# A decode block's weights loaded with two and nine rows per partition, and features taken two apart

## The chip, the cores and the metric

The kernel runs on one core of a Trainium2 chip. The metric is device time in microseconds for one execution: the median of several runs. Times inside a run are microseconds from the start of the profiled span.

## The reference

Four sequences (B = 4) decode one token each. D = 576 features, 32 query heads and 16 key/value heads of 128, of the caches only the last 4096 positions, F = 4608 hidden units. In short:

```python
xn = layernorm(x)
q  = xn @ wq                              # [4, 576] x [576, 4096]
p  = softmax(q . k_cache[last 4096] * 128**-0.5)
o  = p @ v_cache[last 4096]
h  = x + o @ wo                           # [4, 4096] x [4096, 576]
hn = layernorm(h)
g, u = hn @ W_gate, hn @ W_up             # [4, 576] x [576, 4608]
out  = h + (relu(g) * u) @ W_down         # [4, 4608] x [4608, 576]
```

All inputs and the output are bf16. Nearly all the bytes are K and V: 64 pairs of a sequence and a key/value head, 2 MB for two of them.

## The kernel before

Every engine has its program written out by hand (`prog_sync`, `prog_pool`, `prog_act`, `prog_dve`, `prog_pe`). `Sched` turns names of steps into semaphore waits; the order of an engine is the order of its program.

**Transfers.** `transfers` is one list that SP issues in order: wq, then K and V of the 32 "duos" (two heads of one sequence, 2 MB each, K five ahead of V), then wo in 4 pieces, gate and up in alternation, W_down in 9 pieces. All land in one large SBUF tile, `pool`. `add` finds whose place a transfer takes, and SP waits for the last reader of that place before it issues. W_down waits for the step ATTN, the end of the wo matmuls.

**Start.** x is normalised, transposed on TensorE in 5 chunks of features (4 of 128 and one of 64), and multiplied by wq: chunk c of features stands against rows 128c to 128c+127 of wq, which lie one to a partition. The last 64 rows lie as halves on 128 partitions (`xn4`, `hn4` hold the input for them).

**Attention.** For each duo VectorE transposes K (`tr`), TensorE makes scores (`qk`) and, later, P times V (`pv`); four duos form a batch with one softmax.

**End.** The wo matmuls (L578) give h transposed, feature chunk n on partitions, 4 columns for the sequences. After the second norm, gate and up: for each feature chunk c and each of 36 groups of 128 hidden units, one matmul loads a 128x128 block of weights from `pool` as the stationary operand and streams hnT's 4 columns (L595). Which 128 hidden units form group f is told by `cols` (L586): units stand JJ = 3 apart, so that a partition of W_down's tile holds JJ rows that follow one another in memory. Chunk 4 has 18 matmuls for each of gate and up, on halves.

Then h is added to the output in PSUM by multiplying R_sb (h transposed) with an fp32 identity (L610), in pieces along the feature chunks and the two halves of the output (288 columns each, one PSUM bank each). Last come 72 matmuls with W_down as moving operand, 288 columns each (L618), whose pieces are listed in `WD` (L235):

```python
wd_sb = pool[:, 0:FC * D].rearrange("p (g x) -> p g x", g=NG)
WD = [(0, GD * JJ), (GD * JJ, 2 * GD * JJ)] + [(g * JJ, (g + 1) * JJ) for g in range(2 * GD, NG - 1)] + [(FC - JJ, FC - 1), (FC - 1, FC)]
```

that is columns 0-8, 9-17, then 18-20 and so on by threes to 32, then 33-34 and 35. Every matmul and weight load is recorded under L482, the helper `mm`.

Of the kernel before, what the change touches and what calls it, by code (L numbers as in the profile page):

```python
# [12 lines left out]
B = 4  # L13
D = 576
# [6 lines left out]
F = 4608  # L21
FC = F // 128
# [8 lines left out]
DUO = 2 * WIN * DH // 128  # L31
NKS = 4
NVS = 4
ROW = 4608
GU0 = 24064
# [1 line left out]
NKT = 3  # L37
VLEAD = 5
PVLAG = 5
JJ = 3  # L40
GD = 3
BIG = 1.5e38
NG = FC // JJ
HALF = F // 2
HD = D // 2
# [57 lines left out]
def bass_sequential_preLN__sliding_block_cached__glu_gated_reglu__decode_kernel(  # L103
# [12 lines left out]
    with ExitStack() as es:  # L116
        cnt = [0]

        def sb(name, shape, dt):
            return es.enter_context(nc.sbuf_tensor(name, shape, dt))  # L120
# [3 lines left out]
        ident_b = sb("ident_b", [128, 128], BF16)  # L124
        ident_f = sb("ident_f", [128, 128], FP32)
# [13 lines left out]
        oX = sb("oX", [128, 4, H // 4, B], BF16)  # L139
# [22 lines left out]
        R_sb = sb("R_sb", [128, 2, DC, B], FP32)  # L162
# [9 lines left out]
        pb = [sc[:, i * 512:(i + 1) * 512] for i in range(4)]  # L172
        pb += [es.enter_context(nc.psum_tensor(f"pb{i}", [128, 512], FP32))[:, :] for i in range(4, 8)]
        PVB, OB, QB, QR, TPB = 4, 6, 6, 3, 7
        OSB, WOB, STB, GUB, DNB = 0, 1, 2, 7, 4
        tpv = pb[TPB].bitcast(BF16)
# [6 lines left out]
        at = {}  # L183

        def add(name, key, off, n, consumer, make):

            free = []
            for u in list(users):
                if u[0] < off + n and off < u[1]:
                    if u[2] not in free:  # L190
                        free.append(u[2])
                    if off <= u[0] and u[1] <= off + n:
                        users.remove(u)
            users.append((off, off + n, consumer))
            at[name] = off
            transfers.append((name, key, free, lambda e: make(e, pool[:, off:off + n])))
# [13 lines left out]
                lambda e, o: e.dma_start(out=o, in_=duo(A_v_cache, d)))  # L210

        HQ = H * DH
        for c in range(4):
            add(("wq", c), f"wq{c}", NKS * DUO + c * HQ, HQ, "QMM", lambda e, o, c=c: e.dma_start(out=o, in_=A_wq[c * 128:(c + 1) * 128, :]))
        add(("wq", 4), "wq4", NKS * DUO + 4 * HQ, HQ // 2, "QMM",
            lambda e, o: e.dma_start(out=o, in_=A_wq[512:576, :].rearrange("r (u n) -> (r u) n", u=2)))
        for m in range(NDUO + VLEAD):
# [4 lines left out]
        for g in range(NWO):  # L222
            add(("wo", g), f"wo{g}", g * ROW, ROW, "ATTN",
                lambda e, o, g=g: e.dma_start(out=o.rearrange("p (q x) -> p q x", q=2),
                                              in_=A_wo[g * 1024:(g + 1) * 1024, :].rearrange("(q p e) n -> p q (e n)", q=2, e=4)))
        for c in range(4):
            for k, (kind, W) in enumerate((("wg", B_W_gate), ("wu", B_W_up))):
                add((kind, c), f"{kind}{c}", GU0 + (2 * c + k) * ROW, F, None,
                    lambda e, o, c=c, W=W: e.dma_start(out=o, in_=W[c * 128:(c + 1) * 128, :]))
        for u, (kind, W) in enumerate((("wg", B_W_gate), ("wu", B_W_up))):  # L230
            add((kind, 4), f"{kind}4", GU0 + 8 * ROW + u * HALF, HALF, None,
                lambda e, o, W=W: e.dma_start(out=o, in_=W[512:576, :].rearrange("r (u n) -> (r u) n", u=2)))

        wd_sb = pool[:, 0:FC * D].rearrange("p (g x) -> p g x", g=NG)
        WD = [(0, GD * JJ), (GD * JJ, 2 * GD * JJ)] + [(g * JJ, (g + 1) * JJ) for g in range(2 * GD, NG - 1)] + [(FC - JJ, FC - 1), (FC - 1, FC)]  # L235
        for k, (f0, f1) in enumerate(WD):
            g0, j0 = divmod(f0, JJ)
            g1, nj = (f1 // JJ, JJ) if f1 - f0 >= JJ else (g0 + 1, f1 - f0)
            transfers.append((("wd", k), f"wd{k}", ["ATTN"],
                              lambda e, g0=g0, g1=g1, j0=j0, nj=nj: e.dma_start(  # L240
                                  out=wd_sb[:, g0:g1, j0 * D:(j0 + nj) * D],
                                  in_=B_W_down[g0 * 128 * JJ:g1 * 128 * JJ, :].rearrange("(g p j) n -> p g (j n)", p=128, j=JJ)[:, :, j0 * D:(j0 + nj) * D])))

        def land(name):
            return ("L",) + (name if isinstance(name, tuple) else (name,))
# [232 lines left out]
        def prog_pe(S):  # L478
            t = "tensor"

            def mm(o, l, r, start, stop, deps=(), name=None, skip=False):
                S.op(t, lambda e: e.matmul(o, lhsT=l, rhs=r, start=start, stop=stop, skip_group_check=skip),  # L482
                     deps=deps, name=name, signal=name is not None)

            for k, (src, base) in enumerate(((xn_bf, 0), (x_bf, 32))):
                for c in range(DC):
                    w = 128 if c < 4 else 64
                    last = k == 1 and c == DC - 1
                    S.op(t, lambda e, c=c, w=w, src=src, base=base: e.transpose(  # L489
                        out=tpv[0:w, base + c * 4:base + (c + 1) * 4], in_=src[0:B, c * 128:c * 128 + w], identity=ident_b[0:B, 0:B]),  # L490
                        deps=["A_XN", "IDB", land("x")] if k == 0 and c == 0 else [], name="TP1" if last else None, signal=last)
            mm(pb[STB][:, 0:B], dup[:, :], x4[:, :], True, True, deps=["D_XNT", "DUP"], name="XDUP")
            first = True
            for c in range(4):
                s = at[("wq", c)]
                for h in range(H):
                    mm(pb[QB][:, h * B:(h + 1) * B], pool[:, s + h * DH:s + (h + 1) * DH], xnT[:, c, :], first, False,
                       deps=[land(("wq", c))] + (["D_XNT"] if first else []) if h == 0 else [], skip=True)
                    first = False
            s = at[("wq", 4)]  # L500
            for h in range(H // 2):
                o = pb[QB][:, 0:H * B].rearrange("p (u x) -> p u x", u=2)[:, :, h * B:(h + 1) * B]
                mm(o, pool[:, s + h * DH:s + (h + 1) * DH], xn4[:, :, :], False, h == H // 2 - 1,
                   deps=[land(("wq", 4)), "XN41"] if h == 0 else [],
                   name="QMM" if h == H // 2 - 1 else None, skip=True)
            for ce in range(4):
                mm(pb[QR][:, ce * 128:(ce + 1) * 128], sel[:, ce, :, :].rearrange("p g k -> p (g k)"), qT_sb[:, :], True, True,
                   deps=["D_QT", "SEL3"] if ce == 0 else [], name="QREP" if ce == 3 else None)
# [55 lines left out]
            for e_ in range(4):  # L564
                for h4 in range(4):
                    mm(pb[OSB][32 * h4:32 * h4 + 32, e_ * 32:(e_ + 1) * 32], ident_b[:, e_:128:4],
                       oT_all[:, :, :].rearrange("p (q h) b -> p h q b", h=4)[:, h4, :, :], True, True,
                       deps=[("NORM", b) for b in range(B)] if e_ == 0 and h4 == 0 else [],
                       name="OSEL" if e_ == 3 and h4 == 3 else None)
            for g in range(NWO):  # L570
                wv = pool[:, at[("wo", g)]:at[("wo", g)] + ROW].rearrange("p (q e n) -> p q e n", q=2, e=4)
                deps = [land(("wo", g))] + (["D_OX"] if g == 0 else [])
                for n in range(DC):
                    w = 128 if n < 4 else 64
                    for q in range(2):
                        for e_ in range(4):
                            last = g == NWO - 1 and n == DC - 1 and q == 1 and e_ == 3
                            mm(pb[WOB][0:w, n * B:(n + 1) * B], wv[:, q, e_, n * 128:n * 128 + w], oX[:, e_, 2 * g + q, :],  # L578
                               g == 0 and n == 0 and q == 0 and e_ == 0, last, deps=deps, name="ATTN" if last else None, skip=True)
                            deps = []  # L580
            mm(pb[STB][:, 128:168], ones_f[:, :], R_sb[:, :, :, :], True, True, deps=["D_R"], name="STAT")
            mm(pb[STB][:, 256:256 + B], dup[:, :], hnT[0:64, 4, :], True, True, deps=["N2"], name="HDUP")
            first = True
            gub = pb[GUB][:, 0:2 * FC * B].rearrange("p (u x) -> p u x", u=2)

            def cols(ap, fc):  # L586
                g, j = divmod(fc, JJ)
                x0 = g * 128 * JJ + j
                return ap[:, x0:x0 + 127 * JJ + 1:JJ]

            for c in range(4):
                for u, kind in ((0, "wg"), (1, "wu")):
                    s = at[(kind, c)]
                    for f in range(FC):
                        mm(gub[:, u, f * B:(f + 1) * B], cols(pool[:, s:s + F], f), hnT[:, c, :], first, False,  # L595
                           deps=[land((kind, c))] + (["N2"] if first else []) if f == 0 else [], skip=True)
                        first = False
            for u, kind in ((0, "wg"), (1, "wu")):
                o = gub[:, u, :].rearrange("p (v x) -> p v x", v=2)
                for f in range(FC // 2):  # L600
                    last = u == 1 and f == FC // 2 - 1
                    mm(o[:, :, f * B:(f + 1) * B], cols(pool[:, at[(kind, 4)]:at[(kind, 4)] + HALF], f), hn4[:, :, :], False, last,
                       deps=[land((kind, 4)), "HN41"] if f == 0 else [], name=("GU", 4) if last else None, skip=True)
            first = True
            for u in range(2):
                for c in range(DC):
                    lo, hi = max(c * 128, u * HD), min(c * 128 + 128, D, (u + 1) * HD)
                    if lo < hi:
                        w = 128 if c < 4 else 64
                        mm(pb[DNB + u][0:B, lo - u * HD:hi - u * HD], R_sb[0:w, 0, c, :], ident_f[0:w, lo - c * 128:hi - c * 128],  # L610
                           c * 128 <= u * HD, False, deps=["D_R", "IDF"] if u == 0 and c == 0 else [], skip=True)
            for k, (f0, f1) in enumerate(WD):
                deps = [land(("wd", k))] + (["D_HHT"] if k == 0 else [])
                for f in range(f0, f1):
                    g, j = divmod(f, JJ)
                    for u in range(2):
                        last = f == FC - 1
                        mm(pb[DNB + u][0:B, 0:HD], hhT[:, f, :], wd_sb[:, g, j * D + u * HD:j * D + (u + 1) * HD], False, last,  # L618
                           deps=deps, name=f"DOWN{u}" if last else None, skip=True)
                        deps = []  # L620
# [37 lines left out]
```

## Time and profile before

| | |
|---|---|
| median of 3 runs | 384.58 us (384.58 to 385.41) |
| profiled execution | 385.3 us, its span 383.5 us |
| busy share of the span | PE 75%, weight loads 34%, DVE 52%, ACT 13%, POOL 2% |
| DMA | 159.59 MB on SP's queue, 98.6% of 16 engines' span |
| mean rate over the span | 416 GB/s read from HBM |
| granted TensorE clock, mean | 0.907 |

The shares of busy time are averages over four stages (start, attention, wo, gate/up/down). In the first three the transfers run without a break. "PEld" are weight loads, which overlap matmuls; the mean durations of matmuls in a row hold their pipeline, so the pace of a row is read from its length and its count.

### The profile page before, as it was taken

To read this page: it belongs to the slowest core of one execution; us is meant where nothing else is said; L and a number is where in the kernel's file an instruction comes from. 1 tells how busy PE (TensorE), PEld (TensorE's weight loads), DVE (VectorE), ACT (ScalarE), POOL (GpSimd) and SP (SyncE) were. 2 spreads that over 40 slices of the span, in tenths; PEclk is the share of its full clock that TensorE was granted. 3 is DMA by queue.
4 is the path that set the end of the run, shared out by engine and by line. 5 is a ranking of instruction groups with operands and counts; after the bars stand their busy time and mean duration, and the time that the engine had idled before them with its cause. 6 is when DMAs were issued, how large, how long until landed. Compare 5 with 4: busy or idle time off the path is not lost.

```text
span 383.5 us, 4157 instructions
## 1 busy us (share of the span) xinstructions
PE 288.7 (75%) x1827; PEld 130.2 (34%) x1842; DVE 198.8 (52%) x181; ACT 51.5 (13%) x125; POOL 7.9 (2%) x20
## 2 busy tenths in 40 slices
PE   0059649976996699679958994899499788874387
PEld 0053213322432243224322431343134233374355
DVE  0259789269437854774486558645855450011000
ACT  4021040021102110311030004100400021100000
POOL 4000000000000000000000000000000000000000
PEclk9999958998999899989998999899989998955559
DMA  7999999999999999999999999999999999999994
GB/s 316 426 424 426 431 424 432 426 424 431 426 424 434 424 427 431 426 427 431 426 427 434 424 424 434 427 424 432 427 424 434 426 423 434 403 417 424 414 415 172
DMA packets 14306, 159.86 MB, mean 417 GB/s; under 512 B 1480, under 2 KB 1616, under 8 KB 4560
## 3 DMA queue, kind: packets, MB, share of 16 engines
q1 hardware_dynamic: 14280, 159.59, 98.6%
q8 instruction: 14, 0.23, 0.2%
q10 hardware_dynamic: 8, 0.00, 0.0%
q14 instruction: 4, 0.03, 0.0%
HBM read 159.58 MB, written 0.00 MB: 416 GB/s over the span
## 4 chain that ended last, share of the span: by engine, by line
PE 41%; DMA 23%; issue 15%; DVE 14%; ACT 5%; POOL 1%; SPq 0%; POOLq 0%
PE sc L482 23%; PE pb L482 18%; DMA pool<-in_A_k_cache_dram 9%; DMA pool<-in_B_W_down_dram 7%; DMA pool<-in_A_wo_dram 7%; ACT P L323 4%; DVE kT L394 4%; DVE probT L413 4%; DVE rmx L397 4%; POOL bcm L274 1%; DVE bias L409 0%; DVE rowsum L418 0%; DVE t L405 0%; DVE pmax L400 0%; DVE bmin L407 0%
## 5 line engine op out<-in xcount | busy, mean ns | idle before, releaser
L394 DVE STREAM_TRANSPOSE kT<-pool 128x2048 f32<-128x2048 f32 x64 | 144.5, 2291 | 54.6 <-DMA pool<-in_A_k_cache_dram 49.4
L482 PE MATMUL sc<-kT,qz 128*128 128x512 bf16 x497 | 131.9, 418 | 51.2 <-DVE kT L394 47.6
L482 PE MATMUL pb<-pool,prob 128*16 128x512 bf16 x512 | 116.4, 386 | 0.8 <-DMA pool<-in_A_v_cache_dram 0.8
L482 PEld LDWEIGHTS sc<-kT,qz 128*128 128x128 bf16 x512 | 49.0, 102 | 130.9 <-DVE kT L394 57.0
L482 PEld LDWEIGHTS pb<-pool,prob 128*16 128x16 bf16 x512 | 43.5, 91 | 71.0 <-issue 15.3
L323 ACT ACTIVATE P<-sc,bias 128x512 f32<-128x512 f32 x32 | 22.2, 714 | 176.5 <-DVE bias L409 176.5
L397 DVE TENSOR_REDUCE rmx<-sc 128x2 f32<-128x2048 f32 x8 | 18.3, 2292 | 34.0 <-PE sc L482 34.0
L413 DVE STREAM_TRANSPOSE probT<-P 128x2048 f32<-128x2048 f32 x8 | 18.5, 2311 | 7.8 <-ACT P L323 7.8
L482 PE MATMUL pb<-hnT,pool 128*128 128x4 bf16 x288 | 8.8, 167 | 9.8 <-DMA pool<-in_B_W_up_dram 5.0
L489 PE MATMUL pb<-ident_b,xn_bf 4*128 4x4 bf16 (+1 forms) x5 | 0.4, 175 | 20.3 <-ACT xn_bf L287 20.3
L308 ACT COPY cp<-pb 128x512 f32<-128x512 f32 x8 | 4.7, 584 | 67.5 <-PE pb L482 67.5
L482 PEld LDWEIGHTS pb<-hnT,pool 128*128 128x128 bf16 x288 | 8.2, 104 | 10.3 <-DMA pool<-in_B_W_up_dram 5.2
L422 DVE RECIPROCAL rs_sb<-pb 128x32 f32<-128x32 f32 x4 | 1.4, 338 | 19.8 <-PE pb L482 19.8
L482 PE MATMUL pb<-selT,cp 128*128 128x16 f32 x64 | 7.9, 255 | 4.3 <-ACT cp L308 4.3
L473 DVE TENSOR_TENSOR hhT<-pb,gate_sb 128x144 bf16<-128x144 f32 x1 | 0.3, 308 | 20.9 <-ACT gate_sb L339 20.9
L330 ACT CAST prob<-probT 128x1024 bf16<-128x1024 f32 x8 | 8.4, 1044 | 19.0 <-DVE rs L416 19.0
L482 PE MATMUL pb<-pool,hhT 128*4 128x288 bf16 x72 | 10.5, 315 | 0.4 <-DMA pool<-in_B_W_down_dram 0.4
L482 PEld LDWEIGHTS pb<-selT,cp 128*128 128x128 f32 x64 | 8.2, 191 | 6.3 <-ACT cp L308 5.3
L274 POOL PARTITION_ALL_REDUCE bcm<-pmax x8 | 3.1, 386 | 290.6 <-DVE pmax L400 290.6
L301 ACT COPY qz<-qrep 32x64 bf16<-32x64 bf16 x32 | 7.8, 245 | 7.3 <-DVE qrep L431 7.0
L482 PEld LDWEIGHTS pb<-pool,hhT 128*4 128x4 bf16 x72 | 6.6, 93 | 4.3 <-DMA pool<-in_B_W_down_dram 0.7
L489 PEld LDWEIGHTS pb<-ident_b,xn_bf 4*128 4x128 bf16 (+1 forms) x5 | 0.3, 108 | 20.3 <-ACT xn_bf L287 20.3
(94 smaller groups left out, 71.5 us busy)
## 6 DMA issues: line engine op xcount, KB each, us to landing
pool<-in_A_k_cache_dram SPq DMA_DIRECT2D x32, 2048.0 KB, 28.1
pool<-in_A_v_cache_dram SPq DMA_DIRECT2D x32, 2048.0 KB, 26.1
pool<-in_A_wo_dram SPq DMA_DIRECT2D x4, 1152.0 KB, 21.7
pool<-in_B_W_gate_dram SPq DMA_DIRECT2D x4, 1152.0 KB, 25.7
pool<-in_B_W_up_dram SPq DMA_DIRECT2D x4, 1152.0 KB, 24.5
pool<-in_A_wq_dram SPq DMA_DIRECT2D x4, 1024.0 KB, 7.9
pool<-in_B_W_down_dram SPq DMA_DIRECT2D x2, 1296.0 KB, 27.2
pool<-in_B_W_down_dram SPq DMA_DIRECT2D x5, 432.0 KB, 14.5
```

The lines of the kernel that those rows point to most:

```text
L274: S.op(g, lambda e, n=n: e.partition_all_reduce(bcm[:, n % 2, :], pmax[:, n % 2, :], 128, bass_isa.ReduceOp.max), deps=deps, name=("PAR", n))
L301: S.op(a, lambda e, src=src, dst=dst: e.copy(out=dst, in_=src), deps=deps, name=("QZ", n) if g == 3 else None, signal=g == 3)
L308: S.op(a, lambda e: e.copy(out=cp[:, n % 2, :], in_=pb[PVB + n % 2]), deps=deps, name=("CP", n))
L323: S.op(a, lambda e, n=n, th=th, u=u: e.activation(out=P[:, th * 1024 + u:(th + 1) * 1024:2], in_=sc[:, th * 1024 + u:(th + 1) * 1024:2], f ...
L330: S.op(a, lambda e, n=n: e.copy(out=prob[:, n % 2, :, :, :], in_=probT[:, :, 0:NHB].rearrange("p t (r x) -> p r t x", x=4)), deps=deps, na ...
L394: S.op(v, lambda e: e.transpose(out=dst, in_=src), deps=deps, name=("TR", i))
L397: S.op(v, lambda e: e.tensor_reduce(out=rmx[:, n % 2, :], in_=sc[:, :].rearrange("p (x u) -> p u x", u=2), axis=AX.X, op=ALU.max), deps=[( ...
L413: S.op(v, lambda e: e.transpose(out=probT[:, :, :].rearrange("p t j -> p (t j)"), in_=P[:, :]), deps=[("EXP", n, 1)] + ([("CMP", n - 1)] i ...
L422: S.op(v, lambda e: e.reciprocal(out=rs_sb[:, b, :], in_=pb[OB][:, 64 + b * H:64 + (b + 1) * H]), deps=[("SUM", b)], name=("RS", b))
L473: S.op(v, lambda e: e.tensor_tensor(out=hhT[:, :, :], in0=pb[GUB][:, FC * B:2 * FC * B].rearrange("p (f b) -> p f b", b=B), in1=gate_sb[:, ...
L482: S.op(t, lambda e: e.matmul(o, lhsT=l, rhs=r, start=start, stop=stop, skip_group_check=skip), deps=deps, name=name, signal=name is not None)
L489: S.op(t, lambda e, c=c, w=w, src=src, base=base: e.transpose(out=tpv[0:w, base + c * 4:base + (c + 1) * 4], in_=src[0:B, c * 128:c * 128 ...
```

## The change

wq, gate and up are loaded in pairs of chunks: a transfer takes 256 rows, two neighbouring rows on each partition (wq 16384 bytes a partition, gate and up 18432). The feature chunks follow: chunk c of the first four holds features two apart (`feat`), in the transposes of x, in the columns of wo and in the residual matmuls, which write every second column of the output. W_down's tile has JJ = 9 rows a partition instead of 3, so `cols` takes hidden units nine apart, and its pieces are 0-8, 9-17, 18-26, 27-29, 30-32, 33-34, 35. The order of the matmuls is as before, gate and up of chunk c after one another, but both chunks of a pair wait for one landing. The number of matmuls is the same but for the residual, which has seven instead of six.

```diff
-JJ = 3
-GD = 3
+JJ = 9
...
-        for c in range(4):
-            add(("wq", c), f"wq{c}", NKS * DUO + c * HQ, HQ, "QMM", lambda e, o, c=c: e.dma_start(out=o, in_=A_wq[c * 128:(c + 1) * 128, :]))
+        for c in range(2):
+            add(("wq", c), f"wq{c}", NKS * DUO + 2 * c * HQ, 2 * HQ, "QMM",
+                lambda e, o, c=c: e.dma_start(out=o, in_=A_wq[c * 256:(c + 1) * 256, :].rearrange("(p u) n -> p (u n)", u=2)))
...
-        for c in range(4):
+        for c in range(2):
             for k, (kind, W) in enumerate((("wg", B_W_gate), ("wu", B_W_up))):
-                add((kind, c), f"{kind}{c}", GU0 + (2 * c + k) * ROW, F, None,
-                    lambda e, o, c=c, W=W: e.dma_start(out=o, in_=W[c * 128:(c + 1) * 128, :]))
+                add((kind, c), f"{kind}{c}", GU0 + (4 * c + 2 * k) * ROW, 2 * F, None,
+                    lambda e, o, c=c, W=W: e.dma_start(out=o, in_=W[c * 256:(c + 1) * 256, :].rearrange("(p u) n -> p (u n)", u=2)))
...
-        WD = [(0, GD * JJ), (GD * JJ, 2 * GD * JJ)] + [(g * JJ, (g + 1) * JJ) for g in range(2 * GD, NG - 1)] + [(FC - JJ, FC - 1), (FC - 1, FC)]
+        WD = [(0, 9), (9, 18), (18, 27), (27, 30), (30, 33), (33, 35), (35, 36)]
...
+        def feat(c):
+            return slice(c // 2 * 256 + c % 2, c // 2 * 256 + c % 2 + 255, 2) if c < 4 else slice(512, D)
...
-                        out=tpv[0:w, base + c * 4:base + (c + 1) * 4], in_=src[0:B, c * 128:c * 128 + w], identity=ident_b[0:B, 0:B]),
+                        out=tpv[0:w, base + c * 4:base + (c + 1) * 4], in_=src[0:B, feat(c)], identity=ident_b[0:B, 0:B]),
...
-                s = at[("wq", c)]
+                s = at[("wq", c // 2)] + (c % 2) * HQ
...
-                            mm(pb[WOB][0:w, n * B:(n + 1) * B], wv[:, q, e_, n * 128:n * 128 + w], oX[:, e_, 2 * g + q, :],
+                            mm(pb[WOB][0:w, n * B:(n + 1) * B], wv[:, q, e_, feat(n)], oX[:, e_, 2 * g + q, :],
...
-                    s = at[(kind, c)]
+                    s = at[(kind, c // 2)] + (c % 2) * F
                     for f in range(FC):
                         mm(gub[:, u, f * B:(f + 1) * B], cols(pool[:, s:s + F], f), hnT[:, c, :], first, False,
-                           deps=[land((kind, c))] + (["N2"] if first else []) if f == 0 else [], skip=True)
+                           deps=[land((kind, c // 2))] + (["N2"] if first else []) if f == 0 else [], skip=True)
...
-                    lo, hi = max(c * 128, u * HD), min(c * 128 + 128, D, (u + 1) * HD)
-                    if lo < hi:
-                        w = 128 if c < 4 else 64
-                        mm(pb[DNB + u][0:B, lo - u * HD:hi - u * HD], R_sb[0:w, 0, c, :], ident_f[0:w, lo - c * 128:hi - c * 128],
-                           c * 128 <= u * HD, False, deps=["D_R", "IDF"] if u == 0 and c == 0 else [], skip=True)
+                    w = 128 if c < 4 else 64
+                    ds = range(D)[feat(c)]
+                    mine = [p for p in range(w) if u * HD <= ds[p] < (u + 1) * HD]
+                    if mine:
+                        p0, p1 = mine[0], mine[-1] + 1
+                        step = ds.step
+                        o0 = ds[p0] - u * HD
+                        mm(pb[DNB + u][0:B, o0:o0 + step * (p1 - p0 - 1) + 1:step], R_sb[0:w, 0, c, :], ident_f[0:w, p0:p1],
+                           first, False, deps=["D_R", "IDF"] if u == 0 and c == 0 else [], skip=True)
+                        first = False
```

More of the change, by code (lines that the diff above doesn't have):

```diff
@@ L494, in prog_pe @@
             for c in range(4):
-                s = at[("wq", c)]
+                s = at[("wq", c // 2)] + (c % 2) * HQ
                 for h in range(H):
                     mm(pb[QB][:, h * B:(h + 1) * B], pool[:, s + h * DH:s + (h + 1) * DH], xnT[:, c, :], first, False,
-                       deps=[land(("wq", c))] + (["D_XNT"] if first else []) if h == 0 else [], skip=True)
+                       deps=[land(("wq", c // 2))] + (["D_XNT"] if first else []) if h == 0 else [], skip=True)
                     first = False
@@ L603, in prog_pe @@
                        deps=[land((kind, 4)), "HN41"] if f == 0 else [], name=("GU", 4) if last else None, skip=True)
-            first = True
             for u in range(2):
+                first = True
                 for c in range(DC):
-                    lo, hi = max(c * 128, u * HD), min(c * 128 + 128, D, (u + 1) * HD)
-                    if lo < hi:
-                        w = 128 if c < 4 else 64
-                        mm(pb[DNB + u][0:B, lo - u * HD:hi - u * HD], R_sb[0:w, 0, c, :], ident_f[0:w, lo - c * 128:hi - c * 128],
-                           c * 128 <= u * HD, False, deps=["D_R", "IDF"] if u == 0 and c == 0 else [], skip=True)
+                    w = 128 if c < 4 else 64
[8 more added lines that the diff above has]
+                        first = False
             for k, (f0, f1) in enumerate(WD):
```

## The prediction

> **What bounds the kernel now.** I read the page's DMA rows first, then the end of the chain of waits, then the timeline and the windows of the last 20 us. Lines of the page:
>
> ```profile
> PEclk9999958998999899989998999899989998955559
> DMA  7999999999999999999999999999999999999994
> ...
> q1 hardware_dynamic: 14280, 159.59, 98.6%
> ```
>
> The DMA engines are full from the first microseconds to slice 39, so up to the last 20 us the time is bytes over rate. Engines that wait in the attention stage wait for that stream. What follows the stream is seen in the chain of waits (start, length, what):
>
> ```profile
> 343.77 26.88 DMA pool<-in_B_W_down_dram
> 370.64 0.04 issue
> 370.69 10.55 PE pb L482 x72
> 381.24 0.02 issue
> 381.26 0.45 DVE out_sb L475
> ```
>
> The 72 matmuls of W_down start when its first piece lands (370.64) and then run 10.55 us without a wait on any later piece. The timeline shows what PE does just before (start, length, engine, operation; the last bracket is the idle time and what ended it):
>
> ```profile
> 364.66 1.04 PEld L482 LDWEIGHTS pb<-hnT,pool 128*128 128x128 bf16 x36 [1.75 <-DMA pool<-in_B_W_up_dram]
> ...
> 366.10 0.56 PEld L482 LDWEIGHTS pb<-hn,pool 128*128 128x128 bf16 x18 [0.40 <-DMA pool<-in_B_W_gate_dram]
> ...
> 367.52 0.56 PEld L482 LDWEIGHTS pb<-hn,pool 128*128 128x128 bf16 x18 [0.86 <-DMA pool<-in_B_W_up_dram]
> ...
> 368.10 2.17 PE L482 MATMUL pb<-ident_f,R_sb 128*4 128x128 f32 x12
> ```
>
> Gate and up finish 0.6 us after their last landing, the residual matmuls end at 370.27, and only 0.4 us of PE time is left before the first W_down piece. So PE's slack against the stream in this stage is 0.4 us, and behind it PE is the bound. Windows of the same stretch (window, us, PE, PEld, DVE, ACT, POOL, granted clock, DMA share, GB/s):
>
> ```profile
> 200.00:300.00 100.00, 83.81 (x362) 34.09 (x368) 60.04 (x44) 12.32 (x30) 0.77 (x2) 0.95 1.01 428
> 346.00:366.00 20.00, 8.92 (x289) 8.33 (x289) 1.05 (x6) 0.20 (x1) 0.00 (x0) 0.50 1.01 419
> 368.00:376.00 8.00, 7.58 (x50) 4.36 (x48) 0.31 (x1) 0.29 (x1) 0.00 (x0) 0.63 1.03 414
> ...
> 373.00:374.00 1.00, 1.00 (x7) 0.56 (x5) 0.00 (x0) 0.00 (x0) 0.00 (x0) 0.55 1.01 397
> 374.00:375.00 1.00, 1.00 (x10) 0.70 (x9) 0.00 (x0) 0.00 (x0) 0.00 (x0) 1.00 1.02 414
> ...
> 378.00:380.00 2.00, 2.00 (x19) 1.40 (x17) 0.00 (x0) 0.00 (x0) 0.00 (x0) 1.00 0.29 111
> ```
>
> The clock is 0.50 from 337 to 373.9 and 1.00 after it. With c for a W_down matmul at full clock, 3.21/(2c) + 7.34/c = 72 gives c = 0.124 us, and 0.248 at half clock. Its changes in this trace (59.9, 94.0, 373.9) lie 10 and 82 steps of 3.413 us apart, so the next moment at which it could rise is 377.3.
>
> The profiled execution took 385.3 us, 1.8 more than its span; the median is 384.58, 0.7 less. Sums are made against the profiled one, and the difference is carried over to the median.
>
> **Longer rows, so fewer and larger packets.** K and V rows (16 KB) run at 428 GB/s, gate and up (9216 B) at 419, W_down (mostly 3456 B) at 414, wq (8 KB, 6 to 14 us) at 414 in mean. At 428, wq (4.19 MB) saves 0.3 us, the paired gate and up rows (9.44 MB) 0.4 to 0.5, and the 27 of 36 W_down columns that come in nines (3.98 MB) 0.3. The last large up transfer then lands 0.7 us earlier and the middle of W_down 1.0 earlier. Bounds: nothing (longer rows bring none of it) to 1.5 us (wq at 391 in its worst window). I take 0.7 and 1.0.
>
> **Landing granularity.** The wq pairs cost nothing: in the timeline q's matmuls start at 21.43, behind the normalised x (a ScalarE step that ends at 20.20), and all of wq has landed by 15.5. For the first gate and up pair SP now waits for the PV matmuls of duo 28, whose release let the first up transfer go at 327.8; the wo transfer ahead lands at 342.2, so the stream has some 10 us of cover; without it the gap would be idle stream, one for one. Each gate and up pair is needed only when the whole pair is there. The last up pair lands where up 3 lands now, 364.62, less 0.7: 363.9. Behind that landing stand up 2, gate 3, up 3 (36 loads each) and the halves of chunk 4 (18 each), 144 loads instead of 72 with gaps between them. At today's pace, (1.04 - 0.104)/35 = 26.7 ns a load, they take 3.85 us.
>
> **Reading weights 18 bytes apart.** `cols` takes every ninth element instead of every third. q's loads are contiguous and pace at (3.49 - 0.104)/127 = 26.7 ns; gate's, 6 bytes apart, at 26.7 too. No row has 18 bytes. The other end is a load of as many columns without that speed: eight fp32 loads of 128x128 in 0.97 us (mean 191 ns), (0.97 - 0.19)/7 = 111 ns. The ends are 26.7 and 111. I take their middle in ratio, 54 ns. The 6-byte row is nearer, but a step of three times that width can only add, and a loader that delivers 128 columns in 26.7 ns (4.8 a nanosecond, where the fp32 row has 1.2) has most to lose from scattered reads. The 144 loads on the path then take 7.7 us.
>
> [...]
>
> **Features with a stride of two.** The ten transposes of x and wo's 160 loads read 4 bytes apart, between the two steps that show 26.7: nothing, and wo's last 40 matmuls stand behind a landing at 342.16. The residual matmuls become seven instead of six over the same 576 columns and write PSUM 8 bytes apart; today 2.17 us. VectorE's maximum reads PSUM 8 bytes apart, 2048 elements in 2292 ns, as long as its 2048-element transpose from SBUF (2291), so I take 2.2; the other end is a doubling, 4.4. [...]
>
> **W_down in nines.** Columns 18 to 26 come as one piece, which lands where piece 24 to 27 lands now. Between the first piece (370.64) and the last (380.1, its issue at 367.9 plus 12.2 to land) bytes scale to 377.0 for it, less 1.0 gives 376.0. From there 36 matmuls at 0.124 need until 380.4. That is a floor, not the bound, in what follows.
>
> **The sum.** Up pair landed 363.9, plus 7.7 of loads, 0.1 of the last matmul, 2.2 of residual: W_down starts at 373.9 (its data is there). The clock can rise at 377.3: 13.7 matmuls until then, 58.3 at 0.124 after it, end 384.5 against 381.24. That is +3.3 us: 388.6 for the profiled execution, 387.9 for the median.
>
> **Rivals.** (1) *Wide steps cost nothing* (not slower). Loads stay at 26.7 ns: W_down starts at 363.9 + 3.85 + 2.3 = 370.05; with the clock up at 373.9, 15.5 matmuls at half and 56.5 at full clock end at 380.9, that is -0.3: 384.3. For it speaks that contiguous and 6 bytes pace alike; against it, that nothing reaches 18. It decides the sign below about 35 ns a load. (2) *The slow end*, 111 ns: 16.0 us of loads, W_down from 382.2, 10.5 us of it, +11.5: 396.1. For it speaks only that no row excludes it. (3) *The residual's scattered writes double it*, loads at 26.7: start 372.25, end 382.0 or 383.7 by which of the two moments raises the clock: 385.4 to 387.1. (4) *The stream decides*: wide steps are free and the clock is up before W_down starts, as may be so in the median runs, which lie 0.7 below the profiled one. Then the floor counts: 380.4, or less with 1.5 us saved, -0.8 to -1.3: 383.3 to 383.8. (5) *Packets do not grow*: the largest row of before is 16 KB, and rows of 18432 bytes may be cut; that takes 0.4 us from the gain and is inside the other cases.
>
> **How the numbers follow.** A measurement here can tell about 0.3%, 1.15 us, from no change. Forecast (loads of 40 to 75 ns): 0.50, its own range 385.3 to 391.2 (40 ns: start 372.0, end 381.9; 75 ns: start 377.0, clock up at 380.7, end 387.8). Rival 1: 0.32, mostly within 0.3%. Rival 2: 0.09. Rival 3: 0.03. Rival 4: 0.06, the one that is faster. Slower 0.62, same 0.32, faster 0.06. The range reaches from rival 1's value with some of rival 4 down to 384.0, up to 390.7; outside are rival 2, part of rival 4 and the top of the forecast's range.
>
> **What would show it.** In the timeline of after, the LDWEIGHTS group before the residual matmuls: right if its loads stand about 54 ns apart and W_down's chain piece starts near 374 behind PE, not behind a landing. Wrong if a group of 36 still takes 1.04 us. The residual group tells of rival 3 (2.2 or 4.4 us), the window at 346 to 366 of the rates (428 or 419), the chain's last wait of rival 4 (a W_down landing).

## The result, and the profile after

The changed kernel takes 389.29 us (median of 5, 388.63 to 389.70), the kernel before 384.58 (5 runs, 384.55 to 385.41): ratio 1.011, interval 1.0096 to 1.0123. That is 4.7 us slower. The profiled execution took 389.7 us, with a span of 387.9.

The page's lines of after:

```profile
PEclk9999958985998899989998999899999987955559
DMA  8999999999999999999999999999999999999980
q1 hardware_dynamic: 12616, 159.59, 97.2%
```

The bytes are the same in fewer packets (12616 for 14280, 1664 fewer). By the transfers' shapes 1536 rows fewer are read: 256 of wq, 512 of gate and up, 768 of W_down. Had the rows of 18432 bytes come in two packets each, it would be 1024. (The other 128 are packets under 512 bytes, 1480 before and 1352 after.) The DMA engines are now idle in the last slice, while TensorE works on. The end of the chain of waits (start, length, what):

```profile
333.97 29.99 DMA pool<-in_B_W_up_dram
363.97 0.05 issue
364.01 21.62 PE pb L486 x230
385.63 0.02 issue
385.65 0.44 DVE out_sb L479
```

Where the chain came to its last landing at 370.64, with W_down, it now comes there at 363.97, with the last up pair, and TensorE runs from there to the end without a wait: 21.62 us. The timeline shows what it does:

```profile
364.01 6.56 PEld L486 LDWEIGHTS pb<-hnT,pool 128*128 128x128 bf16 x108 [2.44 <-DMA pool<-in_B_W_up_dram]
...
370.47 2.26 PEld L486 LDWEIGHTS pb<-hn,pool 128*128 128x128 bf16 x36
...
372.74 2.17 PE L486 MATMUL pb<-ident_f,R_sb 128*4 128x128 f32 x14
...
374.84 10.77 PE L486 MATMUL pb<-pool,hhT 128*4 128x288 bf16 x72
```

A load takes (6.56 - 0.16)/107 = 60 ns, where it took 26.7. The 144 loads behind the last up landing last from 364.01 to 372.7, the residual is as long as before (2.17 us), and W_down starts at 374.84 instead of 370.69. The windows:

```profile
6.00:14.00 8.00, 0.00 (x0) 0.00 (x0) 0.00 (x0) 0.00 (x0) 0.00 (x0) 1.00 1.01 427
346.00:366.00 20.00, 13.29 (x214) 13.05 (x215) 0.90 (x6) 0.00 (x0) 0.00 (x0) 0.50 1.00 423
378.00:379.00 1.00, 1.00 (x8) 0.59 (x7) 0.00 (x0) 0.00 (x0) 0.00 (x0) 0.73 0.29 107
```

In these profiles wq runs at 427 GB/s (414 before), gate and up at 423 (419), and the last up transfer lands 0.65 us earlier. The rates do not show that longer rows are faster. In the same windows of the other runs below, wq has 420 and 433 where its rows are as before and 423 to 434 where they are paired, and gate and up have 417 to 420 against 416 to 421. The six runs below that also pair gate and up land the last pair between 363.95 and 364.72, where before has 364.62: between 0.67 us earlier and 0.10 later. The clock rises to full within 378 to 379.

### The profile page after: what moved, and what is told of

Same layout as the page of the kernel before. It is cut to its first block, busy times and chain, and to the rows that moved or that the text cites. A ratio compares the mean times of both kernels' runs of the same rounds, so it can differ in the third digit from the quotient of the medians.

```text
span 387.9 us, 4169 instructions
## 1 busy us (share of the span) xinstructions
PE 307.0 (79%) x1844; PEld 142.3 (37%) x1844; DVE 199.1 (51%) x181; ACT 51.6 (13%) x125; POOL 7.9 (2%) x20
## 2 busy tenths in 40 slices
DMA packets 12642, 159.86 MB, mean 412 GB/s; under 512 B 1352, under 2 KB 1488, under 8 KB 3280
## 3 DMA queue, kind: packets, MB, share of 16 engines
q1 hardware_dynamic: 12616, 159.59, 97.2%
## 4 chain that ended last, share of the span: by engine, by line
PE 53%; DVE 17%; issue 15%; DMA 8%; ACT 6%; POOL 1%; POOLq 0%
PE pb L486 28%; PE sc L486 24%; DMA pool<-in_B_W_up_dram 8%; DVE kT L398 6%; ACT P L327 5%; DVE probT L417 4%; DVE rmx L401 4%; POOL bcm L278 1%; DVE bias L413 0%; DVE rowsum L422 0%; DVE t L409 0%; DVE pmax L404 0%; DVE bmin L411 0%; ACT prob L334 0%; ACT qz L305 0%
## 5 line engine op out<-in xcount | busy, mean ns | idle before, releaser
L486 PE MATMUL sc<-kT,qz 128*128 128x512 bf16 x512 | 138.6, 426 | 44.7 <-DVE kT L398 42.9
L486 PE MATMUL pb<-pool,prob 128*16 128x512 bf16 x512 | 117.8, 390 | 0.0
L486 PEld LDWEIGHTS sc<-kT,qz 128*128 128x128 bf16 x512 | 49.6, 103 | 129.6 <-DVE kT L398 53.3
L486 PEld LDWEIGHTS pb<-pool,prob 128*16 128x16 bf16 x512 | 43.9, 91 | 71.7 <-issue 18.1
L486 PE MATMUL pb<-hnT,pool 128*128 128x4 bf16 x288 | 17.8, 199 | 6.0 <-DMA pool<-in_B_W_up_dram 5.5
L486 PEld LDWEIGHTS pb<-hnT,pool 128*128 128x128 bf16 x288 | 17.5, 159 | 6.2 <-DMA pool<-in_B_W_up_dram 5.7
L486 PE MATMUL pb<-selT,cp 128*128 128x16 f32 x64 | 8.7, 269 | 4.3 <-ACT cp L312 4.3
L486 PEld LDWEIGHTS pb<-selT,cp 128*128 128x128 f32 x64 | 9.0, 208 | 6.3 <-ACT cp L312 5.3
L486 PE MATMUL pb<-pool,hhT 128*4 128x288 bf16 x72 | 10.8, 319 | 0.0
L486 PEld LDWEIGHTS pb<-pool,hhT 128*4 128x4 bf16 x72 | 6.7, 94 | 4.0 <-issue 0.2
```

## The experiments

The ratios are to the kernel before in runs on the same chip.

**1. Hidden units three apart, pairs kept** (`e1_step3`).

```diff
-JJ = 9
+JJ = 3
+GD = 3
...
-        WD = [(0, 9), (9, 18), (18, 27), (27, 30), (30, 33), (33, 35), (35, 36)]
+        WD = [(0, GD * JJ), (GD * JJ, 2 * GD * JJ)] + [(g * JJ, (g + 1) * JJ) for g in range(2 * GD, NG - 1)] + [(FC - JJ, FC - 1), (FC - 1, FC)]
```

> The changed kernel with hidden units three apart again (JJ = 3, W_down's pieces as before); the pairs of wq, gate and up and the features two apart stay. Theory (a weight load with columns 18 bytes apart costs 60 ns instead of 26.7, and 144 of them stand behind the last up pair): groups of 36 loads take 1.04 us again, W_down's matmuls start near 370.1 instead of 374.84, and the time is 384.2 us (383.6 to 384.8). Rival (waiting for whole pairs is what costs; the step only shows in the trace): W_down starts later than 372 and the time stays above 387.

Measured 387.01 us, ratio 1.0051 (1.0034 to 1.0069). The loads are at their old pace, but only about half of the loss is gone. The theory's 384.2 us failed, and by its signs the rival came out: W_down starts at 373.33, and the time is above 387. But what stands ahead of W_down is a gap that neither expected. The timeline:

```profile
364.77 2.96 PEld L487 LDWEIGHTS pb<-hnT,pool 128*128 128x128 bf16 x108 [4.51 <-DMA pool<-in_B_W_up_dram]
...
367.65 0.82 PEld L487 LDWEIGHTS pb<-hn,pool 128*128 128x128 bf16 x28
...
370.91 0.29 PEld L487 LDWEIGHTS pb<-hn,pool 128*128 128x128 bf16 x8 [2.44 <-issue]
...
373.33 9.34 PE L487 MATMUL pb<-pool,hhT 128*4 128x288 bf16 x72
```

and the end of the chain of waits:

```profile
364.77 3.79 PE pb L487 x136
368.56 2.35 issue
370.92 11.76 PE pb L487 x94
```

108 loads take 2.96 us (26.7 ns each), then TensorE stops after 28 of chunk 4's 36 loads for 2.35 us, on "issue", that is on nothing the profile shows. Loads of 28 and 8 are no boundary of data: chunk 4 lands in halves of 18. One row of the same run's DMA view, taken for the window 368.3 to 369.6 (packets, MB, share), names a suspect, a transfer on the queue that the profile calls instruction:

```profile
q8 instruction: 1, 0.02, 5.3%
```

The instruction queue, which carries 14 transfers in a whole execution (0.23 MB, so 16 KB each), has one just there. It led to runs 5, 7 and 8.

**2. Gate and up chunk by chunk, hidden units still nine apart** (`e2_single`).

```diff
-        for c in range(2):
+        for c in range(4):
...
-                add((kind, c), f"{kind}{c}", GU0 + (4 * c + 2 * k) * ROW, 2 * F, None,
-                    lambda e, o, c=c, W=W: e.dma_start(out=o, in_=W[c * 256:(c + 1) * 256, :].rearrange("(p u) n -> p (u n)", u=2)))
+                add((kind, c), f"{kind}{c}", GU0 + (2 * c + k) * ROW, F, None,
+                    lambda e, o, c=c, W=W: e.dma_start(out=o, in_=W[c // 2 * 256:(c // 2 + 1) * 256, :].rearrange("(p u) n -> p u n", u=2)[:, c % 2, :]))
...
```

> The changed kernel with gate and up loaded chunk by chunk (one row of 9216 bytes a partition, eight transfers in the order of before); hidden units stay nine apart. Theory (slow loads cost only where they stand behind the last landing, so the pairing is needed for the loss): 72 loads of 60 ns, 4.3 us, follow the landing of up 3 (about 364.3), W_down starts near 370.9, and the time is 385.2 us (384.4 to 386.2). Rival A (the slow loads cost the same however gate and up land): 389. Rival B (the pairing costs nothing, slow loads spread their 10.8 us over the stage): a loss of more than 2 us remains.

Measured 385.39 us, ratio 1.0013 (1.0004 to 1.0022). As the theory has it: the same 60 ns loads, and nearly all of the loss gone. In the timeline 36 loads (2.24 us) end before the next chunk lands, and only 72 stand behind the last landing:

```profile
364.60 2.24 PEld L486 LDWEIGHTS pb<-hnT,pool 128*128 128x128 bf16 x36 [0.57 <-DMA pool<-in_B_W_up_dram]
...
366.74 2.26 PEld L486 LDWEIGHTS pb<-hn,pool 128*128 128x128 bf16 x36
...
371.12 10.55 PE L486 MATMUL pb<-pool,hhT 128*4 128x288 bf16 x72
```

So the wide step adds 10.8 us of loads in the stage (324 loads at 33 ns more) and the kernel is 0.13% slower, as long as most of the loads stand between landings. With run 5, which has the pairs without the wide step, it shows that it takes both to lose 1.1%.

**3 and 4. The pace of a load against its step** (`e3_steps`, `e4_steps`). In the kernel before, gate, up and q read their columns elsewhere; the steps are written in, and a second copy of `mm` on another line (L486) keeps neighbouring groups apart. Both kernels leave the right products out; only the pace of the loads is read. The edit of gate and up, that of q being alike:

```diff
...
-                        mm(gub[:, u, f * B:(f + 1) * B], cols(pool[:, s:s + F], f), hnT[:, c, :], first, False,
+                        MMS[u](gub[:, u, f * B:(f + 1) * B], pool[:, s + f:s + f + 127 * GUSTEP[u][c] + 1:GUSTEP[u][c]], hnT[:, c, :], first, False,
...
```

> The kernel before, in which the weight columns of gate, up and q are read from other places: gate chunks with steps of 1, 2, 4, 5 elements, up chunks with 6, 7, 8, 9, q's chunks (full clock) with 3, 6, 9, 18. It leaves the right products out; only the pace of the loads is read. Theory A (the reader passes over the whole footprint, 8 bytes a turn; 60/26.7 is 9/4): 26.7 ns up to a step of 4, then 6.67 ns times the step: 33, 40, 47, 53, 60. [...]

> As the run before with steps of 10, 12, 16, 18 for gate, 20, 24, 32, 36 for up, and 2, 4, 12, 32 for q at full clock; again the right products are left out. Theory A (whole footprint): 67, 80, 107, 120, 133, 160, 213, 240 ns. [...]

They took 386.68 and 386.77 us, in one run each. The timeline of the first, gate and up (granted clock 0.50 there in before, 337 to 373.8, and in after, 346 to 366), with steps of 2, 4, 5 (L482) and 6, 7, 8, 9 (L486), in the order 6, 2, 7, 4, 8, 5, 9:

```profile
349.58 1.78 PEld L486 LDWEIGHTS pb<-hnT,pool 128*128 128x128 bf16 x36
351.94 1.04 PEld L482 LDWEIGHTS pb<-hnT,pool 128*128 128x128 bf16 x36 [0.58 <-DMA pool<-in_B_W_gate_dram]
354.72 2.01 PEld L486 LDWEIGHTS pb<-hnT,pool 128*128 128x128 bf16 x36 [1.74 <-DMA pool<-in_B_W_up_dram]
357.50 1.25 PEld L482 LDWEIGHTS pb<-hnT,pool 128*128 128x128 bf16 x36 [0.77 <-DMA pool<-in_B_W_gate_dram]
360.30 2.27 PEld L486 LDWEIGHTS pb<-hnT,pool 128*128 128x128 bf16 x36 [1.54 <-DMA pool<-in_B_W_up_dram]
363.07 1.51 PEld L482 LDWEIGHTS pb<-hnT,pool 128*128 128x128 bf16 x36 [0.51 <-DMA pool<-in_B_W_gate_dram]
365.86 2.24 PEld L486 LDWEIGHTS pb<-hnT,pool 128*128 128x128 bf16 x36 [1.28 <-DMA pool<-in_B_W_up_dram]
```

Of the second, steps of 18 (L482) and 36 (L486) as the last two groups:

```profile
363.85 2.31 PEld L482 LDWEIGHTS pb<-hnT,pool 128*128 128x128 bf16 x36 [0.49 <-DMA pool<-in_B_W_gate_dram]
366.64 2.20 PEld L486 LDWEIGHTS pb<-hnT,pool 128*128 128x128 bf16 x36 [0.48 <-DMA pool<-in_B_W_up_dram]
```

With a group's length less one load's mean (0.10 to 0.16 us), over 35:

| step, elements of 2 bytes | 2 | 3 | 4 | 5 | 6 | 7 | 8 | 9 | 18 | 36 |
|---|---|---|---|---|---|---|---|---|---|---|
| ns a load | 26.7 | 26.7 | 32 | 40 | 46 | 53 | 60 | 60 | 61 | 58 |

Theory A falls: 36 has the pace of 8, 58 and 60 ns, where it expected 240. From 4 to 8 the row fits (step + 1) x 6.67 ns within 1.4 ns, and from 8 on it is flat: steps of 10, 12, 16, 20 and 32 in the second run lie between 57 and 61 too. Step 4, 26.7 in theory A, is 32. One group, step 24 in the second run, took 2.58 us (69 ns a load), which stays unexplained. And the granted clock shows no part in it: q's groups, in a stretch where before and after have 1.00 (window 20 to 25), have the same paces. There 32 loads with step 9 take 2.02 us (60 ns) in the first run's timeline:

```profile
23.42 2.02 PEld L482 LDWEIGHTS pb<-xnT,pool 128*128 128x128 bf16 x32
```

and with step 2 0.94 us (27 ns) in the second's:

```profile
20.44 0.94 PEld L482 LDWEIGHTS pb<-xnT,pool 128*128 128x128 bf16 x32
```

**5. The gap of run 1** (`e6_pad`): e1_step3 with 20 small matmuls near the start.

```diff
+            for i in range(20):
+                mm(pb[QR][:, 0:B], dup[:, :], x4[:, :], True, True)
```

> e1_step3 with 20 matmuls of 4 columns put in near the start (40 more instructions on TensorE, results unread). In e1_step3 TensorE stood 2.35 us at 368.56 on nothing that the profile shows, while a 16 KB transfer on the instruction queue began at 368.41. [...] Rival (the gap belongs to chunk 4's loads or their data): it stays at that place, and the time is e1_step3's.

Measured 384.57 us, ratio 0.9991 (0.9978 to 1.0003). The gap is gone, and 2.4 us with it: the rival, by which it stays, is out. From the last landing to the end TensorE runs through, as the chain shows:

```profile
364.23 16.32 PE pb L487 x230
```

W_down starts at 370.26, 3.1 us earlier than in run 1: 2.35 of it is the gap, 0.54 an earlier landing of the last up pair. Its 72 matmuls then take 0.9 us longer (10.27 against 9.34). More work at the start made the kernel faster, which speaks for the place in the instruction stream; runs 7 and 8 try that further.

**6. The residual ahead of gate and up** (`e5_resid`, with the changed kernel's step and pairs).

```diff
+            for u in range(2):
+                first = True
+                for c in range(DC):
...
             mm(pb[STB][:, 256:256 + B], dup[:, :], hnT[0:64, 4, :], True, True, deps=["N2"], name="HDUP")
...
-            for u in range(2):
-                first = True
-                for c in range(DC):
...
             for k, (f0, f1) in enumerate(WD):
```

> The changed kernel with the seven residual matmuls put ahead of gate and up, into TensorE's wait for the second norm. Theory (TensorE is the path from the last up pair to the end): 2.17 us leave the path, some 0.7 us of relu and product come onto it instead, W_down starts near 373.5 instead of 374.84, and the time is 1.4 us below the changed kernel's 389.29, about 1% of before still lost for the most part: 3.3 us above before (2.5 to 4.3). Rival (the path ends with a transfer): no change.

Measured 388.46 us, ratio 1.009 (1.0068 to 1.0112): 3.5 us above before, as expected within its range; 0.8 us won against the 389.29 of the other chip, where 1.4 was expected. The intervals of the two ratios overlap, so the times alone do not show the gain. In the profile W_down starts at 373.88, behind relu (ScalarE) and product (VectorE), 0.96 us earlier, though the last up pair lands 0.2 us later there. That speaks for TensorE as the path.

**7 and 8. The gap again** (`e7_pad4`, `e8_pad10`): as run 5, with 4 and with 10 matmuls.

> e1_step3 with 4 early matmuls of 4 columns put in (8 instructions). [...] Rival (something in chunk 4's own data or landing): 28 and 8 again.

> The same with 10 early matmuls (20 instructions). [...] Rival: 28 and 8, and the gap unchanged.

384.30 and 384.49 us, in one run each; before had 384.78 there. In both the gap is gone, also with 4, where the author expected it 4 loads earlier: a miss. The rival (28 and 8 again) is excluded. In the timeline of the run with 4, chunk 4 runs through:

```profile
367.09 1.04 PEld L487 LDWEIGHTS pb<-hn,pool 128*128 128x128 bf16 x36
```

The DMA view of that run has an instruction transfer in the window 364.1 to 365.4 and none in 368.3 to 369.6; in e1_step3 it is the other way round. So with 8 instructions put in near the start the transfer stands in the window 4.2 us earlier, and there is no gap. The runs show the place and the transfer; by what the transfer would hold TensorE up was not shown. The changed kernel has an instruction transfer in its burst too (window 367.4 to 368.7) and no gap; its 144 loads last 8.7 us, where the 136 pairs ahead of run 1's gap take 3.79.

**9 and 10. Towards a better version** (`v1_step3_resid`: run 1 with run 6's edit; `v2_single_resid`: run 2 with it).

> e1_step3 (hidden units three apart, pairs kept) with the residual matmuls put ahead of gate and up, which also moves the rest by 28 instructions. Theory: no instruction gap behind the last up pair, gate and up end near 368.5, W_down starts with its first piece (370.0 to 370.8), and what is left of the longer rows shows: 0.5 us below before (1.2 below to 0.3 above). Rival (the gap stays): 1 us or more above before.

> e2_single (hidden units nine apart, gate and up chunk by chunk, W_down in nines) with the residual matmuls put ahead of gate and up. Theory: gate and up end near 369.0, relu and product at 369.7, W_down starts with its first piece near 370.5 instead of 371.1: 0.5 us below e2_single, at or slightly below before (1.0 below to 0.4 above). Rival (the end hangs on the clock or the last landing): no change against e2_single.

385.24 us, ratio 1.0005 (0.9992 to 1.0019), and 385.64 us, ratio 1.0015 (1.0002 to 1.0028): no gain. The first lies within its range; the second, 0.64 us above before, misses its range and comes out as its rival said, no different from run 2. In both W_down starts with its first landing, as expected (370.17 and 370.48), but its 72 matmuls then last 10.36 and 11.58 us, where run 1 has 9.34. The window in which the clock rises (granted clock third from the end), of v2_single_resid:

```profile
375.00:376.00 1.00, 1.00 (x6) 0.59 (x5) 0.00 (x0) 0.00 (x0) 0.00 (x0) 0.59 1.00 404
```

and of e1_step3:

```profile
374.00:375.00 1.00, 1.00 (x9) 0.72 (x8) 0.00 (x0) 0.00 (x0) 0.00 (x0) 0.96 1.03 416
```

That is 375.82, 5.3 us after W_down's start at 370.48, in the first, and 374.08, 0.75 us after 373.33, in the second. In these executions, one of each kernel, time that is taken off the path ahead of W_down is given back in part at half clock. No version tried is measurably faster than before; e6_pad's 0.9991 has 1 in its interval.

## Why the prediction was right

**The sum, term by term.** The last up landing: predicted 363.9, measured 363.97. The 144 loads: 7.7 us predicted at 54 ns, 8.7 measured at 60. The residual: 2.2 predicted, 2.17 measured, so its columns two apart in PSUM cost nothing here (14 records, where before has 12), and rival 3 is out. W_down's start: 373.9 predicted, 374.84 measured; all of the difference is the pace of the loads. W_down itself: 10.6 us predicted, 10.77 measured, since 3.7 us of it ran at half clock, to 378.5, and not 3.4, to 377.3. That came out near by luck: the prediction took the moments of before's execution over, and in the twelve profiles the rise lies anywhere from 372.0 to 378.5. The end of the matmuls: 384.5 predicted, 385.6 measured. For the profiled executions that is +4.4 against +3.3; the medians lie 4.7 apart, since after's profiled execution lies 0.4 above its median and before's 0.7, and the prediction carried 0.7 over to both.

**The term that was mis-sized** is the load: 54 ns was the middle in ratio of two far ends, and the runs show 60; no row of before has 18 bytes. That the middle of 26.7 and 111 lay within a tenth of 60 is luck; no row of before told it from either end.

**Rival 1** (wide steps cost nothing, 384.3) was wrong on the step, yet its sum needed a term that nobody had: with cheap loads and pairs (and W_down's pieces as before) the kernel takes 387.0, with the gap of 2.35 us beside the instruction transfer, and only with that gap moved away 384.57. The claim that it "decides the sign below about 35 ns a load" was therefore wrong in this layout. Rival 2 (111 ns) is out with the 60 ns measured. Rival 4 (the stream decides) is out: the chain holds no landing after 363.97. Rival 5 (packets do not grow) is out by the packet count.

**Granularity** was the other half, and the prediction had it as a count (144 loads behind the last landing instead of 72). Run 2 shows it: chunk by chunk the slow loads cost 0.13%. **The longer rows** were to bring the last up landing forward by 0.7 us. The one profile of after has 0.65, but over the seven kernels that pair gate and up it is 0.43 in the mean, with one that lands later than before, and the rates from which the term was worked out do not separate. So this term is not shown, and that it fitted so well is luck. And the rest of the change with the step undone and the gap moved away is not told from before (0.9991).

## What to carry to other kernels

A layout that makes transfers longer may make the reads of the tile wider: look at the step of every access that follows it (here a load took 26.7 ns with 6 bytes between columns and 60 with 18). Slow loads cost what stood of them behind the last landing: 1.1% with 144 there, 0.13% with 72. Pairing the transfers doubled that number, so split the last one. (Run 2 splits them all; the last alone was not tried.) And read "issue" gaps against the DMA view's instruction queue before explaining them by data.

## What the runs showed of the hardware

A weight load of 128 bf16 columns took 26.7 ns with 2 to 6 bytes between columns and 57 to 61 ns with 16 to 72 (one group 69); with 18 bytes it took 60 both in gate and up, at a granted clock of 0.50 in after, and in q (run 3), where before and after have 1.00. An uninterrupted burst of 136 pairs of load and matmul at 26.7 ns ran into a gap of 2.35 us beside an instruction transfer, and with 8 instructions put in earlier there was none. The same 72 matmuls took 9.34 us where the first 0.75 us ran at granted clock 0.50, and 11.58 us where the first 5.3 did.
